# Preparing x one step earlier in a chained Strassen pipeline, with its sums on GpSimd in layer 2

## The chip, the cores and the metric

The kernel runs on one core of a Trainium2 chip. The metric is device time in microseconds (us), the median of three runs. A trace of one further execution, taken by the hardware profiler, is read below. Engines are named as the profile names them: PE is TensorE's matmuls and PEld its weight loads, DVE is VectorE, ACT is ScalarE, POOL is GpSimd, and SP is SyncE, whose queue (SPq) issues the DMAs.

## The reference

The inputs q, k and v are 6016 x 256 in fp32. The first part is attention over channels; two dense blocks of width 2048 follow.

```python
qn = q / (norm(q, axis=1) + 1e-6);  kn = k / (norm(k, axis=1) + 1e-6)
a = softmax(kn.T @ qn / tau)               # 256 x 256
x = v @ a                                  # 6016 x 256
h = x @ w_in1;  g = h - tanh(h);  x = g @ w_out1                                # layer 1
h = x @ w_in2;  g = where(h > 0, h, exp(min(h, 0)) - 1);  out = g @ w_out2      # layer 2
```

## The kernel before

Every fp32 matrix product is made of three fp32r products: a value is split into a high part (ScalarE rounds it to fp32r) and a low part (value minus high part, mostly on GpSimd), and high x high, high x low and low x high are summed in PSUM. The attention matrix is folded into w_in1 first, so layer 1 reads v itself.

Tokens are cut into 12 blocks of 512 (the last has 384). In the code `layer` is 0 for layer 1 and 1 for layer 2; a phase is one (layer, block). A phase has eight steps p = 0 to 7, one for each 256 columns of the 2048. From layer 1's block 3 on, the loop `for i in range(len(todo) + LAG)` (line 1084) takes one step per turn and writes out by hand, in program order, what each engine gets. Every engine runs its own list in that order.

**A step on TensorE.** A step is either "plain" (24 matmuls of 512 columns for h) or "seven" (`Step.seven`): one Strassen level, seven products of 3 matmuls each of 256 columns: `one`, `two`, `six`, `five`, `four`, `three`, `seventh`. Layer 2 is plain at p = 1 and 5, layer 1 at p = 4. The products that begin with a chain accumulate in one PSUM bank `qa`; ScalarE copies intermediate states of it (`copy`, line 776), and `four` and `three` of a step run inside the next step (`finish`). Then VectorE reads the end of the chain (`close_chain`, line 793 in layer 2), which frees `qa`; `merge` (line 780) and `close` (line 786) free `qb`. There are two `qa` and two `qb`. Between these products lie 12 matmuls of 512 columns (line 935) that multiply the finished g of a step four (layer 1) or five (layer 2) turns back by w_out.

**The activation.** In layer 2 ScalarE makes tanh (line 815) and exp (line 810), VectorE `begin` (line 822) and `end` (line 830), ScalarE the high part `ghi` (line 837), GpSimd the low part `glo` (line 840). GpSimd has `glo` in every step; short pieces of other work are put behind it (`pool_end`).

**x's parts and sums for the next phase.** While a phase runs, the next block of x is prepared out of one tile `vraw` (one buffer, filled by `load_v`, line 249, at p = 0):

- `split_v_scalar` (ScalarE, line 256): high part `vhi`, at p = 1
- `half_of_lower` (GpSimd, line 690): low part `vlo`, a half at p = 2 and a half at p = 3
- `sum_v` (VectorE, lines 666 to 668): the Strassen sums, written in place over `vraw`, at p = 4, ahead of the step's `close_chain` on VectorE
- `sum_v_scalar` (ScalarE, line 674): their high part `thi`, at p = 4 in layer 1 and p = 5 in layer 2
- `half_of_sums_lower` (GpSimd, line 702): their low part `tlo`, at p = 5 and 6 in layer 1, and p = 6 and 7 in layer 2

The next block's first `six` reads `thi` and `tlo`. `load_v` must wait until the last `tlo` of the phase before has read `vraw`.

**Other pieces that the change touches.** `fetch_sums(i + 1)` (line 1093) issues, at the head of a turn, the load of the weights' Strassen sums `ws` (three buffers, line 657) for the next turn, on SP's queue in program order with all other loads and stores. `emit_evac` (lines 949 to 971) copies a block's two finished accumulators out of PSUM into the two halves of one tile `osb`: the first by ScalarE (line 963), the second by VectorE (line 961) where b > 2, by ScalarE otherwise; then it stores the tile. In layer 1's block 3, `own_sums` (VectorE, line 650) makes layer 1's weight sums for p = 0, 2, 4, 6 at the even steps; ScalarE's cast of them (line 638) is in the same step, the low part and the store (lines 641 and 642) in the step behind it.

Of the kernel before, what the change touches and what calls it, by code (L numbers as in the profile page):

```python
# [8 lines left out]
F32 = mybir.dt.float32  # L9
F32R = mybir.dt.float32r  # L10
# [12 lines left out]
def kernel(  # L23
# [501 lines left out]
    with tc.manual_schedule():  # L525
# [14 lines left out]
        late_stack = ExitStack()  # L540


        next_w = opool.tile([P, 2, width], F32R, tag="osb", name="next_w")
        next_w = [next_w[:, :, : 2 * P], next_w[:, :, 2 * P :]]
        early.aside[1] = next_w

        def fold_attention(p):
# [111 lines left out]

        t_of = {}  # L660

        def sum_v(i, raw):

            x = halves(raw)
            tt = nc.vector.tensor_tensor
            tt(out=x[:, 0:2], in0=x[:, 1:4:2], in1=x[:, 0:2], op=ALU.subtract)
            tt(out=x[:, 3], in0=x[:, 3], in1=x[:, 0], op=ALU.subtract)
            tt(out=x[:, 2], in0=x[:, 2], in1=x[:, 3], op=ALU.subtract)
            t_of[i] = x

        def sum_v_scalar(i):
# [11 lines left out]
        def half_of_lower(i, k):  # L683

            n = blocks[phases[i][1]][1]
            if k == 0:
                lower_of[0] = vpool.tile([P, KC, width], F32R, tag="vlo", name=f"vlo{i}")
            raw, hi = v_of[i][:2]
            lo = lower_of[0]
            nc.gpsimd.tensor_tensor(  # L690
                out=lo[:, k, :n], in0=raw[:, k, :n], in1=hi[:, k, :n].bitcast(F32), op=ALU.subtract
            )
            if k == 1:
                v_of[i] = (hi, lo)
# [254 lines left out]
        def emit_evac(layer, b, p):  # L949
            if p < NP - 1:  # L950
                return
            t0, n = blocks[b]
            o = o_of.pop((layer, b))
            s = opool.tile([P, 2, width], F32, tag="osb", name="osb")[:, :, :n]
            for c in range(KC):
                to, of = s[:, c], o[c][:, :n]
                if layer == 0:
                    to = to.rearrange("p (h q u) -> p h u q", h=2, q=16)
                    of = of.rearrange("p (h u q) -> p h u q", h=2, q=16)
                if c and b > 2:  # L960
                    nc.vector.tensor_copy(out=to, in_=of)  # L961
                else:
                    nc.scalar.activation(out=to, in_=of, func=AF.Copy)  # L963
                if (layer, b) == phases[-1]:
                    nc.sync.dma_start(out=outT[c * P : (c + 1) * P, t0 : t0 + n], in_=s[:, c])
            if layer == 0:
                nc.sync.dma_start(out=x_dram[b], in_=s)
            elif (layer, b) != phases[-1]:
                nc.sync.dma_start(
                    out=outT[:, t0 : t0 + n].rearrange("(k p) t -> p k t", p=P), in_=s  # L970
                )

        order = [(0, b, p) for p in range(NP) for b in range(2)]
        order += [(layer, b, p) for layer, b in phases[2:] for p in range(NP)]
# [46 lines left out]
        for s, (layer, b, p) in list(enumerate(order))[2 * NP : 3 * NP]:  # L1021
            h = emit_h(layer, b, p)
            done = pend.pop(0)
            emit_out(*done)
            work = []
            if p == 3:
                work.append(lambda: split_v_rest(nv, nc.vector))
            if p == 5:
                work.append(lambda: sum_v(nv, raw_of[0]))
            if p == 7:  # L1030
                work.append(lambda: sum_v_rest(nv, nc.vector))
            if own_left:
                work.append(own_left.pop()[1])
            if p in OWN:
                work.append(lambda: own_sums(2 * OWN.index(p) + 1))
            pend.append((layer, b, p, emit_act(layer, b, p, h, None, convert=p == 0, work=work)))
            emit_evac(*done[:3])
            if own_left:
                own_left[0][0]()
            if p == 0:  # L1040
                load_v(nv)
                raw_of[0] = v_of[nv]
            if p == 2:
                split_v_scalar(nv)
            if p == 5:
                sum_v_scalar(nv)
            if p == 7:
                nv += 1
# [11 lines left out]
        def fetch_sums(i):  # L1060
            if i < len(todo) and strassen(*todo[i]):
                layer, _, p = todo[i]
                sums_at[i] = load_sums(layer, p)
# [20 lines left out]
        for i in range(len(todo) + LAG):  # L1084
# [4 lines left out]
            if i < len(todo):  # L1089
                layer, b, p = todo[i]  # L1090
                cur = Step(layer, b, p, sums_at.pop(i, None))
                steps.append(cur)
                fetch_sums(i + 1)
                if p == 0 and nv < len(phases):
                    load_v(nv)
                    raw_of[0] = v_of[nv]
# [19 lines left out]
            before_act, after_act, scalar_mid, scalar_end, pool_end = [], [], [], [], []  # L1116
            if cur and nv < len(phases):
                apart = strassen(*phases[nv], 3)
                if p == 1:
                    scalar_end.append(lambda: split_v_scalar(nv))  # L1120
                if p in (2, 3):
                    pool_end.append(lambda: half_of_lower(nv, p - 2))
                if p == 4 and apart:
                    before_act.append(lambda: sum_v(nv, raw_of[0]))
                if p == 4 + layer and apart:
                    (scalar_mid if layer else scalar_end).append(lambda: sum_v_scalar(nv))
                if p in (5 + layer, 6 + layer) and apart:
                    pool_end.append(lambda: half_of_sums_lower(nv, p - 5 - layer))
            if cur and layer == 0 and b == 3:
                if own_left:  # L1130
                    before_act.append(own_left.pop()[1])
                if p % 2 == 0:
                    before_act.append(lambda: own_sums(p))
                    scalar_end.append(lambda: own_left[0][0]())
            if cur and layer == 0 and b > 3:
                vector, scalar, pool = conversion(i)
                after_act += vector
# [35 lines left out]
            if cur is None:  # L1173
                if two:
                    two.tanh()
                vector_begin()
                out(6)
                finish()
            elif cur.seven:
                cur.one()  # L1180
                cur.copy(0)
                cur.two()
                if two:
                    two.tanh()
                vector_begin()
                out(6)
                cur.six()
                cur.copy(2)
                cur.five()
                finish()  # L1190
            else:
                cur.plain(0)
                cur.plain_copy(0)
                if two:
                    two.tanh()
                vector_begin()
                if boundary:
                    finish()
                    out(6)
                else:  # L1200
                    out(6)
                    finish()
            act_b()
            if cur is None:
                out(12)
# [66 lines left out]
```

## Time and profile before

| | before |
|---|---|
| median of three runs | 1138.6 us (1138.21 to 1140.17) |
| profiled execution, its own time | 1141.42 us |
| its span, first to last instruction | 1139.6 us |
| PE busy | 1050.6 us, 92% |
| DVE, ACT, POOL busy | 73%, 70%, 53% |
| mean granted TensorE clock | 0.97 of full speed |

Busy time is an average over stages. The loop over steps begins at 181 us (layer 1's block 3) and enters layer 2 at 557 us; but for `next_w`, the change lies behind 181 us.

### The profile page before, as it was taken

Reading aid. Unit: us, or ns where it says so; the run is one execution under the profiler, and the core shown is the slowest. Engines: PE = TensorE matmul, PEld = TensorE weight load, DVE = VectorE, ACT = ScalarE, POOL = GpSimd, SP = SyncE. Lnnn points to the kernel's source line nnn. Section 1 sums busy time; section 2 is a strip of 40 time slices with the busy share of each in tenths; the row PEclk is TensorE's granted clock in tenths of the full one; section 3 lists DMA queues with packets and bytes.
Section 4 is the critical chain, followed back from the end, with each engine's and each line's share of the span. In section 5 each row is a group of like instructions: output and inputs, shape, how many; then the busy total and the mean of one; then the engine's idle time right before and its main releaser. Section 6 shows DMA issues by size and latency. Waiting matters only on the chain. (4 is left out here: it accounts for less than half of the span.)

```text
span 1139.6 us, 16167 instructions
## 1 busy us (share of the span) xinstructions
PE 1050.6 (92%) x6025; PEld 947.3 (83%) x6025; DVE 834.2 (73%) x1047; ACT 797.6 (70%) x1230; POOL 609.7 (53%) x336
## 2 busy tenths in 40 slices
PE   9999999899999999999878988989889898898998
PEld 8888887789889889889868887888878888787897
DVE  7899977766666766755477867868767686876886
ACT  7877665578778778776466766767766676665775
POOL 4522101576777776676535655555655455654552
PEclk9999999999999999999889999999989999998999
DMA  9633023355455545553842222322221422223200
GB/s 362 222 110 120 10 102 115 127 193 175 153 181 167 177 174 167 171 182 96 284 174 74 74 74 98 125 75 74 74 89 60 139 84 74 74 74 125 74 1 33
DMA packets 66750, 141.29 MB, mean 124 GB/s; under 512 B 5360, under 2 KB 27120, under 8 KB 66672
## 3 DMA queue, kind: packets, MB, share of 16 engines
q1 hardware_dynamic: 66384, 139.74, 35.8%
q8 instruction: 47, 0.77, 0.3%
q10 hardware_dynamic: 288, 0.52, 0.1%
q14 instruction: 31, 0.25, 0.1%
HBM read 112.20 MB, written 28.05 MB: 123 GB/s over the span
## 5 line engine op out<-in xcount | busy, mean ns | idle before, releaser
L840 POOL TENSOR_TENSOR glo<-g,ghi 128x1024 fp32r<-128x1024 f32 (+1 forms) x165 | 420.2, 2547 | 418.4 <-ACT ghi L837 332.5
L935 PE MATMUL o<-ghi,wout 128*128 128x512 f32 (+1 forms) x1472 | 379.7, 384 | 1.8 <-DVE osb L961 1.2
L935 PEld LDWEIGHTS o<-ghi,wout 128*128 128x128 f32 x1472 | 263.4, 195 | 26.4 <-DVE osb L961 1.5
L776 ACT ACTIVATE copies<-qa 128x256 f32<-128x256 f32 x357 | 135.4, 380 | 154.8 <-PE qa L746 154.0
L837 ACT ACTIVATE ghi<-g 128x1024 fp32r<-128x1024 f32 (+1 forms) x168 | 173.6, 1034 | 64.8 <-DVE g L826 58.6
L935 PE MATMUL o<-glo,wout 128*128 128x512 f32 (+1 forms) x736 | 211.2, 384 | 0.0
L830 DVE SCALAR_TENSOR_TENSOR g<-g,hs 128x1024 f32<-128x1024 f32 (+1 forms) x96 | 168.1, 1751 | 1.8
L826 DVE TENSOR_TENSOR g<-hs,e 128x1024 f32<-128x1024 f32 (+1 forms) x72 | 85.7, 1190 | 92.8 <-ACT e L818 83.0
L935 PEld LDWEIGHTS o<-glo,wout 128*128 128x128 f32 x736 | 133.2, 195 | 13.1
L822 DVE SCALAR_TENSOR_TENSOR g<-e,g 128x1024 f32<-128x1024 f32 (+1 forms) x96 | 115.1, 1199 | 39.1 <-ACT e L810 39.0
L746 PE MATMUL qa<-thi,ws 128*128 128x256 f32 x476 | 122.9, 282 | 8.0 <-ACT copies L776 4.2
L746 PEld LDWEIGHTS qa<-thi,ws 128*128 128x128 f32 x476 | 93.3, 196 | 19.2 <-ACT copies L776 8.0
L780 DVE TENSOR_TENSOR hs<-qb,copies 128x512 f32<-128x512 f32 x119 | 81.4, 684 | 28.7 <-ACT copies L776 28.7
L815 ACT ACTIVATE g<-hs 128x1024 f32<-128x1024 f32 (+1 forms) x96 | 99.5, 1036 | 0.0
L810 ACT ACTIVATE e<-hs 128x1024 f32<-128x1024 f32 (+1 forms) x96 | 96.5, 1005 | 0.0
L746 PE MATMUL qa<-tlo,ws 128*128 128x256 f32 x238 | 68.4, 288 | 30.0 <-POOL tlo L702 30.0
L283 PE MATMUL qa<-vhi,win 128*128 128x512 f32 (+1 forms) x196 | 68.4, 391 | 22.7 <-DVE hs L793 22.7
L793 DVE COPY hs<-qa 128x256 f32<-128x256 f32 x66 | 27.9, 422 | 75.4 <-PE qa L746 75.4
L746 PEld LDWEIGHTS qa<-tlo,ws 128*128 128x128 f32 x238 | 46.5, 195 | 38.5 <-POOL tlo L702 32.9
L746 PE MATMUL qb<-vhi,ws 128*128 128x256 f32 x238 | 65.8, 300 | 11.7 <-DVE hs L780 11.5
L818 ACT ACTIVATE e<-hs 128x1024 f32<-128x1024 f32 (+1 forms) x72 | 72.2, 1002 | 0.0
L746 PE MATMUL qb<-vhi,win 128*128 128x256 f32 x238 | 60.7, 281 | 4.8 <-DVE hs L786 4.8
(168 smaller groups left out, 2182.4 us busy)
## 6 DMA issues: line engine op xcount, KB each, us to landing
ws<-sums SPq DMA_DIRECT2D x119, 512.0 KB, 4.2
sums<-sums_out SPq DMA_DIRECT2D x14, 512.0 KB, 2.9
qk<-in_q_dram SPq DMA_DIRECT2D x23, 256.0 KB, 5.0
vraw<-in_vT_dram SPq DMA_DIRECT2D x11, 512.0 KB, 4.7
x<-osb SPq DMA_DIRECT2D x11, 512.0 KB, 2.6
vraw<-x SPq DMA_DIRECT2D x11, 512.0 KB, 3.5
out_dram<-osb SPq DMA_DIRECT2D x11, 512.0 KB, 3.0
qk<-in_k_dram SPq DMA_DIRECT2D x21, 256.0 KB, 5.2
```

Source lines behind the costliest of these rows:

```text
L746: nc.tensor.matmul(out=out, lhsT=w, rhs=x, start=start and k == 0, stop=k == 2, skip_group_check=True,)
L776: nc.scalar.activation(out=self.copies[:, k], in_=self.qa[:, :W], func=AF.Copy)
L780: nc.vector.tensor_tensor(out=self.hs[:, 0:4:3], in0=self.qb.rearrange("p (a t) -> p a t", a=2), in1=self.copies[:, 0:2], op=ALU.add,)
L810: nc.scalar.activation(out=self.e, in_=self.h, func=AF.Exp)
L815: nc.scalar.activation(out=self.g, in_=self.h, func=AF.Tanh, scale=0.5)
L818: nc.scalar.activation(out=self.e, in_=self.h, func=AF.Tanh)
L822: nc.vector.scalar_tensor_tensor(out=self.g, in0=self.e, scalar=1.0, in1=self.g, op0=ALU.add, op1=ALU.mult)
L826: nc.vector.tensor_tensor(out=self.g, in0=self.h, in1=self.e, op=ALU.subtract)
L830: nc.vector.scalar_tensor_tensor(out=self.g, in0=self.g, scalar=0.0, in1=self.h, op0=ALU.min, op1=ALU.max)
L837: nc.scalar.activation(out=self.hi, in_=self.g, func=AF.Copy)
L840: (engine or nc.gpsimd).tensor_tensor(out=self.lo, in0=self.g, in1=self.hi.bitcast(F32), op=ALU.subtract)
L935: nc.tensor.matmul(out=columns(o[c][:, :n]), lhsT=w[:, f, c * P : (c + 1) * P], rhs=turned(x[:, i]), start=(f == 0 and w is wout_hi and x ...
```

## The change

Six edits. (1) In both layers `split_v_scalar` goes from p = 1 to p = 0 and the two `vlo` halves from p = 2, 3 to p = 1, 2. (2) In layer 2 `sum_v` leaves VectorE (p = 4) for GpSimd, its first instruction at p = 3 and the other two at p = 4; `thi` stays at p = 5, now behind the step's `ghi`; the `tlo` halves go from p = 6, 7 to p = 5, 6. In layer 1 the sums keep their engine and place. (3) `fetch_sums` asks for the step after next, in the middle of a turn, once the product `three` of the step before is issued. (4) The accumulators are copied into two tiles, one for each half, and each is stored by a DMA of its own. (5) In layer 1's block 3 `own_sums` goes from the even to the odd steps. (6) An early weight tile `next_w` is made of two tiles, since it shares the pool.

```diff
@@ weights used by the first fold
-        next_w = opool.tile([P, 2, width], F32R, tag="osb", name="next_w")
-        next_w = [next_w[:, :, : 2 * P], next_w[:, :, 2 * P :]]
+        next_w = [opool.tile([P, width], F32R, tag=f"osb{k}", name=f"next_w{k}") for k in range(2)]
+        next_w = [w.rearrange("p (c f) -> p c f", c=KC) for w in next_w]
@@ sum_v
-        def sum_v(i, raw):
+        def sum_v(i, raw, engine, parts):
             x = halves(raw)
-            tt = nc.vector.tensor_tensor
-            tt(out=x[:, 0:2], in0=x[:, 1:4:2], in1=x[:, 0:2], op=ALU.subtract)
-            tt(out=x[:, 3], in0=x[:, 3], in1=x[:, 0], op=ALU.subtract)
-            tt(out=x[:, 2], in0=x[:, 2], in1=x[:, 3], op=ALU.subtract)
+            tt = engine.tensor_tensor
+            if 0 in parts:
+                tt(out=x[:, 0:2], in0=x[:, 1:4:2], in1=x[:, 0:2], op=ALU.subtract)
+            if 1 in parts:
+                tt(out=x[:, 3], in0=x[:, 3], in1=x[:, 0], op=ALU.subtract)
+                tt(out=x[:, 2], in0=x[:, 2], in1=x[:, 3], op=ALU.subtract)
@@ emit_evac
-            s = opool.tile([P, 2, width], F32, tag="osb", name="osb")[:, :, :n]
+            s = [opool.tile([P, width], F32, tag=f"osb{c}", name=f"osb{c}")[:, :n] for c in range(KC)]
...
-                if (layer, b) == phases[-1]:
-                    nc.sync.dma_start(out=outT[c * P : (c + 1) * P, t0 : t0 + n], in_=s[:, c])
-            if layer == 0:
-                nc.sync.dma_start(out=x_dram[b], in_=s)
...
+                if layer == 0:
+                    nc.sync.dma_start(out=x_dram[b][:, c], in_=s[c])
+                else:
+                    nc.sync.dma_start(out=outT[c * P : (c + 1) * P, t0 : t0 + n], in_=s[c])
@@ the loop over steps
-                fetch_sums(i + 1)
+                if i == 0:
+                    fetch_sums(1)
...
-                if p == 1:
+                if p == 0:
                     scalar_end.append(lambda: split_v_scalar(nv))
-                if p in (2, 3):
-                    pool_end.append(lambda: half_of_lower(nv, p - 2))
-                if p == 4 and apart:
-                    before_act.append(lambda: sum_v(nv, raw_of[0]))
+                if p in (1, 2):
+                    pool_end.append(lambda: half_of_lower(nv, p - 1))
+                if layer == 0 and p == 4 and apart:
+                    before_act.append(lambda: sum_v(nv, raw_of[0], nc.vector, (0, 1)))
+                if layer == 1 and p in (3, 4) and apart:
+                    pool_end.append(lambda: sum_v(nv, raw_of[0], nc.gpsimd, (p - 3,)))
                 if p == 4 + layer and apart:
-                    (scalar_mid if layer else scalar_end).append(lambda: sum_v_scalar(nv))
-                if p in (5 + layer, 6 + layer) and apart:
-                    pool_end.append(lambda: half_of_sums_lower(nv, p - 5 - layer))
-            if cur and layer == 0 and b == 3:
-                if own_left:
-                    before_act.append(own_left.pop()[1])
-                if p % 2 == 0:
-                    before_act.append(lambda: own_sums(p))
-                    scalar_end.append(lambda: own_left[0][0]())
+                    scalar_end.append(lambda: sum_v_scalar(nv))
+                if p in (5, 6) and apart:
+                    pool_end.append(lambda: half_of_sums_lower(nv, p - 5))
+            if own_left:
+                before_act.append(own_left.pop()[1])
+            if cur and layer == 0 and b == 3 and p % 2 == 1:
+                before_act.append(lambda: own_sums(p - 1))
+                scalar_end.append(lambda: own_left[0][0]())
@@ behind the step's products and `finish`, ahead of `act_b`
+            if cur:
+                fetch_sums(i + 2)
             act_b()
```

## Rows read from the trace of the kernel before

**Rows 1.** The page, first part: busy time of each engine.

```profile
PE 1050.6 (92%) x6025; PEld 947.3 (83%) x6025; DVE 834.2 (73%) x1047; ACT 797.6 (70%) x1230; POOL 609.7 (53%) x336
```

**Rows 2.** Windows: stretch, its us, busy us by engine, granted clock, DMA.

```profile
181.00:557.30 376.30, 357.38 (x2182) 324.00 (x2182) 249.43 (x374) 277.07 (x498) 248.54 (x164) 1.00 0.51 169
557.30:1088.70 531.40, 470.61 (x2692) 424.85 (x2691) 387.02 (x429) 356.54 (x517) 294.87 (x130) 0.94 0.27 94
...
660.90:664.30 3.40, 3.40 (x15) 3.25 (x16) 1.12 (x3) 1.30 (x2) 0.00 (x0) 0.55 0.69 255
664.30:685.20 20.90, 20.90 (x130) 19.11 (x128) 17.23 (x17) 16.44 (x24) 13.20 (x6) 1.00 0.18 60
```

**Rows 3.** Waits of PE: who for whom; us in total, times, longest.

```profile
PE qa L746 <- POOL tlo L702: 30.0, 10, 3.0
PE qa L283 <- DVE hs L793: 22.7, 10, 5.7
PE qb L746 <- DVE hs L780: 11.5, 14, 1.1
PE qa L746 <- ACT copies L776: 5.0, 5, 1.8
PE qb L746 <- DVE hs L786: 4.8, 12, 1.3
PE qa L746 <- DMA ws<-sums: 3.5, 2, 3.1
```

**Rows 4.** Timeline where layer 2's block 2 begins: start, us, engine.

```profile
655.00 1.29 POOL L702 TENSOR_TENSOR tlo<-vraw,thi 128x512 fp32r<-128x512 f32 x1
...
655.62 0.27 PE L746 MATMUL qa<-vhi,win 128*128 128x256 f32 x1
...
659.54 1.26 POOL L702 TENSOR_TENSOR tlo<-vraw,thi 128x512 fp32r<-128x512 f32 x1
660.83 0.32 SPq L249 DMA_DIRECT2D vraw<-x  x1
...
660.86 0.58 PE L746 MATMUL qa<-tlo,ws 128*128 128x256 f32 x1 [3.00 <-POOL tlo L702]
```

**Rows 5.** Timeline of DVE at p = 4 of that block.

```profile
682.60 2.26 DVE L666 TENSOR_TENSOR vraw<-vraw 128x512 f32<-128x512 f32 x1
...
686.83 0.42 DVE L793 COPY hs<-qa 128x256 f32<-128x256 f32 x1
```

**Rows 6.** Tile vraw: its users' ns (min/median/max), its DMAs.

```profile
L702 POOL TENSOR_TENSOR tlo<-vraw,thi x36: 1252/1278/1737, 217.1 to 1045.6; 128x512 fp32r<-128x512 f32 x36
...
L666 DVE TENSOR_TENSOR vraw<-vraw x19: 683/2259/2268, 170.9 to 1019.8; 128x512 f32<-128x512 f32 x19
L667 DVE TENSOR_TENSOR vraw<-vraw x19: 424/426/2546, 171.6 to 1023.2; 128x256 f32<-128x256 f32 x19
...
DMA to landing us min/median/max: 3.1/4.4/7.5
```

**Rows 7.** Timelines of POOL and of DVE at one moment of layer 2.

```profile
694.31 2.38 POOL L840 TENSOR_TENSOR glo<-g,ghi 128x1024 fp32r<-128x1024 f32 x1 [4.33 <-issue]
...
694.43 3.33 DVE L830 SCALAR_TENSOR_TENSOR g<-g,hs 128x1024 f32<-128x1024 f32 x1
```

**Rows 8.** Timelines of ACT, DVE and PE where layer 1's accumulators leave PSUM.

```profile
245.93 1.08 ACT L963 ACTIVATE osb<-o 128x512 f32<-128x512 f32 x1
...
247.04 1.04 DVE L961 COPY osb<-o 128x512 f32<-128x512 f32 x1 [0.88 <-ACT osb L963]
...
248.66 0.38 PE L746 MATMUL qb<-vhi,ws 128*128 128x256 f32 x1 [1.14 <-DVE hs L780]
```

**Rows 9.** Timeline of ACT at the start of layer 1's block 3.

```profile
185.68 0.63 ACT L638 ACTIVATE sums_out<-sum 128x512 fp32r<-128x512 f32 x1 [2.53 <-DMA sums<-sums_out]
```

**Rows 10.** Timelines of SP and ACT at p = 0 in layer 1.

```profile
269.38 0.45 SPq L249 DMA_DIRECT2D vraw<-in_vT_dram  x1
...
273.50 0.41 ACT L203 ACTIVATE out<-cut 128x256 fp32r<-128x256 f32 x1
```

More of the change, by code (lines that the diff above doesn't have):

```diff
@@ L953, in emit_evac @@
             o = o_of.pop((layer, b))
-            s = opool.tile([P, 2, width], F32, tag="osb", name="osb")[:, :, :n]
+            s = [opool.tile([P, width], F32, tag=f"osb{c}", name=f"osb{c}")[:, :n] for c in range(KC)]
             for c in range(KC):
-                to, of = s[:, c], o[c][:, :n]
+                to, of = s[c], o[c][:, :n]
                 if layer == 0:
@@ L963, in emit_evac @@
                     nc.scalar.activation(out=to, in_=of, func=AF.Copy)
-                if (layer, b) == phases[-1]:
-                    nc.sync.dma_start(out=outT[c * P : (c + 1) * P, t0 : t0 + n], in_=s[:, c])
-            if layer == 0:
-                nc.sync.dma_start(out=x_dram[b], in_=s)
[L968 to L971, printed above, removed]
+                if layer == 0:
+                    nc.sync.dma_start(out=x_dram[b][:, c], in_=s[c])
+                else:
+                    nc.sync.dma_start(out=outT[c * P : (c + 1) * P, t0 : t0 + n], in_=s[c])
         order = [(0, b, p) for p in range(NP) for b in range(2)]
@@ L1028 @@
             if p == 5:
-                work.append(lambda: sum_v(nv, raw_of[0]))
+                work.append(lambda: sum_v(nv, raw_of[0], nc.vector, (0, 1)))
             if p == 7:
```

## The prediction, made before the changed kernel ran

> **What bounds the kernel now.** First the page: TensorE is busy for 92% of the span, the next engine for 73% [rows 1]. So only what makes TensorE wait, or slows its clock, can change the time. The windows say where that is [rows 2]. Layer 1's part of the loop takes 376.3 us with 357.4 of them busy, at full clock. Layer 2's eleven full blocks take 531.4 us with 470.6 busy, so 60.8 us idle, and the granted clock there is 0.94: 531.4 x 0.06 = 31.9 us are lost to it. Idle and clock are one story. In 660.90 to 664.30, right behind a wait of 3.0 us (below), the grant is 0.55, nearly all at 1.2 GHz; in the next 20.9 us, with no wait, it is 1.00 (2.4 GHz) and TensorE is busy throughout [rows 2]. So a layer 2 block is 531.4 / 11 = 48.3 us, of which 5.5 are waits and 2.9 clock; 39.9 us is what it would take without either.
>
> Then the list of TensorE's waits [rows 3]: 30.0 us for `tlo` from GpSimd, ten times 3.0, once a block; 22.7 us for the release of `qa` by VectorE (line 793), ten times; the rest is small. The two large ones are nearly all of the 60.8.
>
> The timelines give their causes. The next block's step 0 begins at 655.62; its `six` wants `tlo` at 657.86 (the wait of 3.00 before 660.86), but the second half of `tlo` ends at 660.80, while the first half had ended at 656.29 [rows 4]. The reload of `vraw` is issued the moment `tlo` is done (660.83), so the loop load, `vhi`, `vlo`, sums, `thi`, `tlo` sets the block's period. The other wait: at p = 4 `sum_v` begins on VectorE at 682.60 and `close_chain`, queued behind it, at 686.83 [rows 5]; the plain step p = 5 then has no `qa`.
>
> **The change part by part.**
>
> *`tlo` one step earlier.* The second half takes the place that the first half has now: ready at about step 0 + 0.67 us (656.29 - 655.62), wanted at + 2.24. The wait of 30.0 us goes, with 1.6 us to spare. Bounds: 0 and 30.0; I take 30.0.
>
> *`sum_v` off VectorE in layer 2.* `close_chain` at p = 4 no longer has 4.2 us of queue ahead of it: -22.7 us (bounds 0 and 22.7). What follows from these waits goes as well: of the 11.5 us at line 780, 3.5 lie in layer 2 (seven layer 1 waits of about 1.14 make the other 8.0), and I take 3.0.
>
> What GpSimd pays: one subtraction of 512 columns at 1.28 us, like `tlo` [rows 6], and two of 256. These have no row here; between half of 1.28 and all of it they cost 0.64 to 1.28 each, and I take 0.75, because the work is half: 2.8 us a block, bounds 2.6 and 3.8. GpSimd is busy 13.2 of 20.9 us in the clean stretch, so there is room in it. But it gets short pieces in six steps in a row (p = 1 to 6), while the clean stretch has two.
>
> The price is in sharing. At 694.31 `glo` starts on GpSimd and ends at 696.69; `end` on VectorE, issued at 694.43, ends at 697.76, so it ran in the 1.1 us behind GpSimd's instruction [rows 7]: these two exclude each other. Counted as exclusive, a block needs 8 x (2.38 + 1.1) for `glo` and `end`, 4 x 1.28 for the halves and 2.8 for the sums, 35.8 of 39.9 us. VectorE's own sums took 0.68 + 2 x 0.42 = 1.5 when alone and up to 2.27 + 2.55 when not [rows 6], so the shared load rises by about 1.3 us. It fits, with 10% left. For new small waits of TensorE I take 0.85 us a block, 9.5 us in eleven: the lower bound is zero (the clean stretch), the upper 2.2 us a block, one `end` held behind a whole `glo` (3.33 - 1.1).
>
> The Trainium skill speaks against this edit twice. "SBUF — State Buffer", section "Who interferes with whom", says that a VectorE instruction with two SBUF inputs and a GpSimd instruction that reads SBUF block each other for the whole instruction; rows 7 agree (2.2 us of blocking). "GPSIMD Engine Reference", section "4.1 Engine selection", gives two-input elementwise work to VectorE, with GpSimd about 2x slower; that would be 3.0 us a block by the 1.5 alone, against my 2.8, and moves the sum by 2 us.
>
> *The clock.* One stretch like 660.90 to 664.30 costs 3.4 x 0.45 = 1.5 us [rows 2]. If the waits go, these go: of 31.9 us I take 28 (bounds 0 and 31.9), since layer 2's first steps keep some waits.
>
> *`fetch_sums` two ahead.* `ws` has three buffers, and a buffer comes free at the same product `three` either way, so in steady state the load starts no earlier. It does where other loads stand between: the 3.1 us wait at layer 2's start [rows 3]. I take 2.1 (bounds 0 and 3.5).
>
> *`osb` in two tiles.* VectorE's copy waited 0.88 us for ScalarE's copy into the other half of the same tile, and TensorE then waited 1.14 for `merge` [rows 8]. With two tiles both run side by side: 7 x 0.88 = 6.2 us in layer 1 (bounds 0 and 8.0). One more DMA issue on SP a block has nothing late behind it.
>
> *`vlo` earlier and `own_sums` at odd steps, layer 1.* VectorE's sums no longer wait for `vlo`, and at an odd step no `close` is queued behind `own_sums`: of the 4.8 us at line 786 I take 4.0. At block 3's start ScalarE stands 2.53 us for the store of the one `sums_out` tile [rows 9], and `copy` behind it costs TensorE 1.8 [rows 3]; the cast moves a step back, so -1.8.
>
> *`vhi` at p = 0.* Here the edit can cost. The load of `vraw` is issued at 269.38, and ScalarE comes to the pieces at the end of p = 0 at 273.50, 4.1 us later [rows 10]; loads land in 3.1 to 7.5 us, median 4.4 [rows 6]. ScalarE then waits about 0.3 us, and `copy` and `ghi` are queued behind it, for which TensorE and GpSimd wait. I take 1.5 us in seven blocks; the upper bound is 7 x 3.4 = 24.
>
> *Sum.* -30.0 - 22.7 - 3.0 - 28 - 2.1 - 6.2 - 4.0 - 1.8 = -97.8; + 9.5 + 1.5 = +11.0; net -86.8. The profiled execution took 1141.4, 2.8 above the runs' median: 1141.4 - 86.8 = 1054.6, less 2.8, is **1052 us**. Every gain at its bound and every price at zero gives about 1030.
>
> **The rivals.**
>
> *A: `tlo` stays late, by less.* With six pieces in a row GpSimd could slip by one `glo` and its piece, 2.4 + 1.3 = 3.7 us, against 1.6 to spare: 2.1 us late in ten blocks, 21 us, and a half-clock stretch of 1.5 behind half of them, 8 us: 1052 + 29 = 1081. For: GpSimd is in order and has never had more than two pieces in a row in layer 2. Against: its idle time in the clean stretch. Chance 0.15.
>
> *B: VectorE is held behind GpSimd.* `end` behind a whole `glo` in three steps of each block, 3 x 2.2 = 6.6 us; some 2.5 of it absorbed (VectorE is idle 3.7 of 20.9 us in the clean stretch), 4 us a block left, 44 in all, in place of my 9.5: 1052 + 35 = 1087, and with a half-clock stretch in each block 1103. Chance 0.13. (The Trainium skill's page "SBUF — State Buffer", in the section named above, states this blocking; the prices are those of rows 7.)
>
> *C, slower: ScalarE stalls on the load of `vraw`.* If the load lands late at p = 0 in every block, everything behind it on ScalarE is late. At 7.5 us it is 7.5 - 4.1 = 3.4 late in layer 1 [rows 6, 10], and at most as late in layer 2: 18 x 3.4 = 61 us, and 18 half-clock stretches of 1.5, 27 us. These 88 us take the whole gain: 1140. Each further microsecond of landing is 18 us, so at 8.5 it is 1158. For: 7.5 was seen. Against: the median is 4.4. Chance 0.05.
>
> *D: smoother than I allow*, below 1034. Chance 0.07.
>
> **How the numbers follow.** The forecast's own range, 1034 to 1070, has 0.60. Up to 1098 lie A (0.15) as well and about half of B (0.06): 0.81 in all. D (0.07) is left out below, B's upper half and C (0.12) above. Range 1034 to 1098. About 0.2% (2.3 us) is what a measurement of this kernel can tell from no change. The forecast, A, B and D are all faster, 0.95; of C I give 0.01 to no change and 0.04 to slower.
>
> **What would show it.** Right: no wait of `six` for `tlo`; no wait of the plain step for line 793; clock at 0.99 or more in layer 2; layer 2 blocks of 40 to 42 us; `osb` on VectorE without the 0.88 us; waits at line 780 of 0.3 us in layer 1. A would show as `tlo` waits of 1 to 2 us, B as waits on lines 780 and 793 with `end` at 3 us and longer, C as ScalarE idle at line 256 for a DMA. The prediction fails if any one of these recurs every block, since each brings the lower clock with it.

## The result and the profile after

The changed kernel takes 1070.9 us (1068.86 to 1071.79, four runs) beside 1139.4 (1138.21 to 1140.17) for the kernel before: ratio 0.9397, interval 0.938 to 0.9414. The forecast was 1052, its range 1034 to 1098; the time is 0.9 us above the forecast's own range, which ended at 1070.

The profiled execution took 1070.94 us with a span of 1069.1. Its page, first part, as in [rows 1] (line numbers from `sum_v` on are two higher than before: `merge` 782, `close` 788, `end` 832, `glo` 842, `osb` 963 and 965):

```profile
PE 1022.9 (96%) x6025; PEld 926.9 (87%) x6025; DVE 819.0 (77%) x1017; ACT 796.3 (74%) x1230; POOL 663.7 (62%) x366
```

Its windows, layer 1's part of the loop and layer 2's eleven full blocks, as the first two of [rows 2]:

```profile
180.91:565.48 384.57, 360.46 (x2183) 326.12 (x2182) 256.86 (x374) 277.84 (x498) 249.81 (x164) 0.99 0.50 164
565.48:1018.00 452.52, 439.87 (x2690) 402.58 (x2690) 366.11 (x399) 354.15 (x517) 346.86 (x160) 1.00 0.32 111
```

Read against [rows 2]: layer 2 fell by 531.40 - 452.52 = 78.9 us, layer 1 rose by 384.57 - 376.30 = 8.3, together -70.6, and the profiled executions differ by 70.5. The forecast's terms, sorted the same way, were -76.3 for layer 2 (`tlo`, line 793, line 780, clock, `ws`, less the 9.5 of new waits) and -10.5 for layer 1 (`osb`, line 786, the cast, less the 1.5 for `vhi`). So layer 1 is 18.8 us worse than forecast and layer 2 is 2.6 better, which makes the 16.3 (but for rounding) by which the profiled execution lies above the 1054.6 of the sum. The other 2.5 of the error come from the 2.8 that the forecast took off because the profiled execution before lay above the median; the one after lies at it.

TensorE's list of waits after, as [rows 3] (us in total, times, longest):

```profile
PE qb L748 <- DVE hs L782: 15.2, 18, 2.0
PE qa L748 <- ACT copies L778: 13.6, 11, 5.1
PE qb L748 <- DVE hs L788: 4.1, 7, 1.8
...
PE qa L748 <- DMA ws<-sums: 0.3, 1, 0.3
```

The two large waits of before, 30.0 us for `tlo` and 22.7 for line 793, are not in it. In layer 2 TensorE's idle time fell from 531.40 - 470.61 = 60.8 us to 452.52 - 439.87 = 12.7, and its busy time, at a higher clock, from 470.6 to 439.9. What leads it now, `merge` and `copy`, is to two thirds in layer 1. The same list for the stretch of layer 1 alone (180 to 566 us of after, 180 to 558 of before):

```profile
PE qa L748 <- ACT copies L778: 11.6, 9, 5.1
PE qb L748 <- DVE hs L782: 7.9, 7, 1.1
PE qb L748 <- DVE hs L788: 2.2, 6, 0.9
```

```profile
PE qb L746 <- DVE hs L780: 7.9, 7, 1.1
PE qb L746 <- DVE hs L786: 4.8, 12, 1.3
PE qa L746 <- ACT copies L776: 3.6, 4, 1.8
```

Line 788 gave 2.6 us, not 4.0. The wait for `merge`, which the split of `osb` was to remove, has not moved at all: 7.9 us in seven, before and after. The wait for ScalarE's `copy` grew from 3.6 to 11.6.

Layer 1 in time: its first stretch, from the loop's start to the point where ScalarE copies block 3's accumulators (245.93 in [rows 8]), before and after:

```profile
181.00:245.93 64.93, 58.51 (x332) 51.19 (x332) 45.99 (x66) 41.33 (x71) 32.94 (x21) 0.97 0.43 146
180.91:253.81 72.90, 60.81 (x332) 53.32 (x332) 51.10 (x66) 41.47 (x71) 33.04 (x21) 0.93 0.40 138
```

This stretch alone lost 8.0 of the 8.3 us; the rest of layer 1 took 311.4 us before and 311.7 after.

A step 0 in layer 2, timeline of GpSimd and TensorE (beginning, us, instruction; what it waited for in brackets):

```profile
687.46 3.45 POOL L842 TENSOR_TENSOR glo<-g,ghi 128x1024 fp32r<-128x1024 f32 x1 [0.30 <-ACT ghi L839]
690.87 1.28 POOL L704 TENSOR_TENSOR tlo<-vraw,thi 128x512 fp32r<-128x512 f32 x1
...
691.44 0.27 PE L748 MATMUL qa<-vhi,win 128*128 128x256 f32 x1
...
693.51 0.28 PE L748 MATMUL qa<-tlo,ws 128*128 128x256 f32 x1
```

The second half of `tlo` is ready at 692.15, step 0 + 0.71 us (forecast: + 0.67), and `six` takes it at + 2.07 without a wait.

Layer 1, timelines of SP, ScalarE, VectorE, GpSimd and TensorE, in order of time:

```profile
183.45 0.72 SPq L249 DMA_DIRECT2D vraw<-in_vT_dram  x1
...
189.37 1.06 ACT L256 ACTIVATE vhi<-vraw 128x1024 fp32r<-128x1024 f32 x1 [6.26 <-DMA vraw<-in_vT_dram]
190.75 0.58 PE L748 MATMUL qa<-thi,ws 128*128 128x256 f32 x1 [5.07 <-ACT copies L778]
...
201.14 2.60 POOL L842 TENSOR_TENSOR glo<-g,ghi 128x1024 fp32r<-128x1024 f32 x1 [9.32 <-ACT ghi L839]
201.54 3.62 DVE L630 TENSOR_TENSOR sum<-whole 128x128 f32<-128x128 f32 x2
...
208.24 0.38 PE L748 MATMUL qa<-thi,win 128*128 128x256 f32 x1 [2.39 <-ACT copies L778]
...
253.81 1.07 ACT L965 ACTIVATE osb<-o 128x512 f32<-128x512 f32 x1 [0.27 <-PE o L937]
254.91 1.04 DVE L963 COPY osb<-o 128x512 f32<-128x512 f32 x1 [0.85 <-ACT osb L965]
256.53 0.38 PE L748 MATMUL qb<-vhi,ws 128*128 128x256 f32 x1 [1.13 <-DVE hs L782]
```

Three suspects are to be seen in it, and the runs below test each. In block 3, the loop's first, ScalarE comes to `vhi` at 189.37 - 6.26 = 183.11, 0.34 us before the load of `vraw` is even issued; it stands 6.26 us for it, and TensorE 5.07 us for the `copy` queued behind. At 201.54 VectorE's weight sums (`own_sums`), now at an odd step, run together with `glo` on GpSimd, and TensorE is 2.39 us late at 208.24. And VectorE's `osb` copy still waits 0.85 us for ScalarE's, though they write different SBUF tiles now.

### The profile page after: what moved, and what is told of

The parts are those of the page before. It is cut to its first block, busy times and chain, and to the rows that moved or that the text cites. A ratio compares the mean times of both kernels' runs of the same rounds, so it can differ in the third digit from the quotient of the medians.

```text
span 1069.1 us, 16198 instructions
## 1 busy us (share of the span) xinstructions
PE 1022.9 (96%) x6025; PEld 926.9 (87%) x6025; DVE 819.0 (77%) x1017; ACT 796.3 (74%) x1230; POOL 663.7 (62%) x366
## 4 chain that ended last, share of the span: by engine, by line
PE 74%; DVE 9%; ACT 6%; DMA 4%; issue 3%; POOL 3%; SPq 0%; ACTq 0%; DVEq 0%; POOLq 0%
PE o L937 36%; PE qa L748 12%; PE qb L748 10%; PE h L283 5%; PE qb L283 4%; PE qa L283 3%; PE S L351 3%; DVE g L828 2%; POOL glo L842 1%; DMA qk<-in_k_dram 1%; ACT ghi L839 1%; ACT osb L965 1%; DVE g L832 1%; ACT e L820 1%; DVE sum L630 1%
## 5 line engine op out<-in xcount | busy, mean ns | idle before, releaser
L937 PE MATMUL o<-ghi,wout 128*128 128x512 f32 (+1 forms) x1472 | 374.6, 380 | 1.8 <-DVE osb L963 1.2
L937 PEld LDWEIGHTS o<-ghi,wout 128*128 128x128 f32 x1472 | 259.2, 191 | 25.7 <-DVE osb L963 1.5
L937 PE MATMUL o<-glo,wout 128*128 128x512 f32 (+1 forms) x736 | 207.6, 379 | 0.0
L832 DVE SCALAR_TENSOR_TENSOR g<-g,hs 128x1024 f32<-128x1024 f32 (+1 forms) x96 | 177.1, 1845 | 1.8
L937 PEld LDWEIGHTS o<-glo,wout 128*128 128x128 f32 x736 | 130.4, 191 | 12.7
L692 POOL TENSOR_TENSOR vlo<-vraw,vhi 128x512 fp32r<-128x512 f32 (+1 forms) x40 | 62.0, 1550 | 46.2 <-ACT vhi L256 46.2
L748 PE MATMUL qb<-vhi,ws 128*128 128x256 f32 x238 | 61.3, 284 | 15.4 <-DVE hs L782 15.2
L283 PE MATMUL qa<-vhi,win 128*128 128x512 f32 (+1 forms) x196 | 63.2, 363 | 0.0
L283 PE MATMUL qb<-vhi,win 128*128 128x512 f32 (+1 forms) x196 | 63.0, 363 | 0.0
```

Source lines behind the costliest of these rows:

```text
L283: nc.tensor.matmul(out=out, lhsT=w, rhs=x, start=(i == 0), stop=(i == len(pairs) - 1))
L748: nc.tensor.matmul(out=out, lhsT=w, rhs=x, start=start and k == 0, stop=k == 2, skip_group_check=True,)
L832: nc.vector.scalar_tensor_tensor(out=self.g, in0=self.g, scalar=0.0, in1=self.h, op0=ALU.min, op1=ALU.max)
L937: nc.tensor.matmul(out=columns(o[c][:, :n]), lhsT=w[:, f, c * P : (c + 1) * P], rhs=turned(x[:, i]), start=(f == 0 and w is wout_hi and x ...
```

## The experiments

All start from the changed kernel unless it is said otherwise; the lengths of the layers are read from the timeline of TensorE, as the windows above. Each length is that of one execution, which can lie some us from its kernel's median (3.3 below it in e2, 2.4 above it in e3).

**e1: `vhi` of layer 1 back at p = 1.** Theory: `vhi` at p = 0 costs layer 1 what the load of `vraw` is late.

```diff
-                if p == 0:
+                late = 1 - layer
+                if p == late:
-                if p in (1, 2):
-                    pool_end.append(lambda: half_of_lower(nv, p - 1))
+                if p - late in (1, 2):
+                    pool_end.append(lambda: half_of_lower(nv, p - late - 1))
```

> The changed kernel (1070.9 us), but in layer 1 x's high part is again made at p = 1 and the low halves at p = 2 and 3; layer 2 keeps the new places. Theory: in layer 1 ScalarE reaches the piece at p = 0 ahead of the load of vraw (6.3 us of standing at block 3, 8.2 us in all), and what is queued behind it holds up TensorE (5.07 us at 190.75, 0.2 to 0.4 us in each later block). So the time falls by 6 to 9 us, to 1062 to 1065, with ScalarE no longer idle for the load, and the small waits at close (0.2 to 0.5 us a block) come back. Rival: layer 1 lost its 8 us through own_sums at the odd steps, and the load's wait is covered by TensorE's own slack: within 2 us of 1070.9.

Measured 1065.7 us, ratio to before 0.9345 (0.9322 to 0.9367): 5.1 us faster than the change, and the intervals lie apart. In layer 1 the waits for `copy` fall from 11.6 us in nine to 4.5 in two. Its first and its last stretch, and TensorE where the wait of 5.07 us was:

```profile
181.33:250.04 68.71, 60.93 (x333) 53.75 (x333) 50.31 (x66) 41.74 (x71) 32.78 (x21) 0.93 0.43 146
543.90:563.60 19.70, 17.38 (x96) 17.08 (x96) 11.15 (x14) 10.32 (x16) 12.82 (x9) 0.91 0.76 253
```

```profile
188.29 0.35 PE L748 MATMUL qa<-thi,ws 128*128 128x256 f32 x1 [2.19 <-issue]
```

The first stretch is 4.2 us shorter than after the change (72.90). The last is 2.8 longer (16.9 in the change): TensorE waits 2.3 us in place of 1.2 for an `osb` copy there, and the clock is 0.91. So layer 1 as a whole gains 2.3; layer 2, which this edit doesn't touch, is 2.7 shorter, with one wait of 2.0 us for `merge` fewer.

**e2: `own_sums` back at even steps.**

```diff
-            if cur and layer == 0 and b == 3 and p % 2 == 1:
-                before_act.append(lambda: own_sums(p - 1))
+            if cur and layer == 0 and b == 3 and p % 2 == 0:
+                before_act.append(lambda: own_sums(p))
```

> The changed kernel, but own_sums is again at the even steps of block 3. Theory: at the odd steps the sums on VectorE stand behind GpSimd's glo and piece (3.6 us for two subtractions of 128 columns that take 0.5 when alone), VectorE comes late to begin, ScalarE to ghi, and the copy behind that holds TensorE 2.4 us and 2.2 us. At the even steps these two waits go and those of before at close (0.9 and 1.3 us) come back: 1 to 4 us faster than 1070.9. Rival: the place of own_sums only moves the same wait from one name to another: within 1 us.

Measured 1069.7, ratio 0.9378 (0.935 to 0.9407): not told apart from the change. In the trace the wait of 2.39 us falls to 0.76, as before the change, and one of 1.26 for `close`, gone with the change, is back; the first stretch of layer 1 is 2.9 us shorter.

**e3: the two accumulators in two PSUM tiles.** Theory: the two `osb` copies are in order because both read one PSUM tile `o`, so splitting `osb` alone does nothing.

```diff
-                o = (ps_b if (layer, b) == (0, 1) else ps_o).tile(
-                    [P, KC, 512], F32, tag="o", name=f"o{layer}_{b}"
-                )
-                o_of[layer, b] = [o[:, 0], o[:, 1], o]
+                if (layer, b) == (0, 1):
+                    o = ps_b.tile([P, KC, 512], F32, tag="o", name=f"o{layer}_{b}")
+                    o_of[layer, b] = [o[:, 0], o[:, 1]]
+                else:
+                    o_of[layer, b] = [
+                        ps_o.tile([P, 512], F32, tag=f"o{c}", name=f"o{c}_{layer}_{b}") for c in range(KC)
+                    ]
```

> The changed kernel, with the two accumulators o in two PSUM tiles of a bank each instead of one tile of two banks (the SBUF copies are apart already). Theory: VectorE's copy still waits 0.85 us for ScalarE's because both read one PSUM tile, not because they wrote one SBUF tile; with two tiles the wait is gone, merge comes 0.85 us earlier and the 1.13 us waits of layer 1 fall to about 0.3: 6 us faster in layer 1, up to 3 us in layer 2, 1062 to 1066. Rival: the order between the two copies has another cause (the products of both accumulators end together and VectorE itself is not free before): no change, 1069 to 1072, with VectorE still idle until ScalarE's copy ends.

Measured 1076.0, ratio 0.9435 (0.9408 to 0.9461): all four runs above all four of the change (the intervals just touch). VectorE's wait for ScalarE's copy is gone (0.85 us in layer 1, 0.63 in layer 2) and layer 1 is 4.5 us shorter, so the theory of the wait holds; its time, 1062 to 1066, doesn't, because layer 2 takes 12.3 us more: 3.8 of waits and 8.5 of TensorE's busy time, at a clock of 0.97. Window and timeline of e3 in layer 2 (lines three higher than after):

```profile
561.26:1026.12 464.86, 448.39 (x2689) 410.18 (x2689) 357.96 (x399) 354.33 (x517) 343.58 (x160) 0.97 0.31 108
```

```profile
804.09 2.38 POOL L845 TENSOR_TENSOR glo<-g,ghi 128x1024 fp32r<-128x1024 f32 x1 [0.27 <-ACT ghi L842]
804.12 3.42 DVE L835 SCALAR_TENSOR_TENSOR g<-g,hs 128x1024 f32<-128x1024 f32 x1
807.47 0.68 DVE L785 TENSOR_TENSOR hs<-qb,copies 128x512 f32<-128x512 f32 x1
808.21 0.38 PE L751 MATMUL qb<-vhi,ws 128*128 128x256 f32 x1 [1.99 <-DVE hs L785]
```

The same step of the same block after the change:

```profile
808.61 1.23 DVE L832 SCALAR_TENSOR_TENSOR g<-g,hs 128x1024 f32<-128x1024 f32 x1
808.67 3.40 POOL L842 TENSOR_TENSOR glo<-g,ghi 128x1024 fp32r<-128x1024 f32 x1 [0.47 <-ACT ghi L839]
```

There `end` begins 0.06 us ahead of `glo`, takes 1.23 us, and `glo` pays with 3.40. In e3 `end` begins 0.03 us after `glo` and takes 3.42, `merge` is late behind it, and TensorE waits 1.99 us. This stands in six of the eleven blocks (in two after the change): rival B's mechanism, called up by an `osb` copy that ended 0.63 us sooner two steps earlier. (The Trainium skill, "SBUF — State Buffer", section "Who interferes with whom", states that such a pair blocks each other for the whole instruction; the 3.42 us agree.)

**e4, e5: layer 2's sums on VectorE.** e4 puts all three ahead of `close_chain` at p = 4, as before the change, with everything else kept; e5 at the ends of p = 3 and p = 4, where GpSimd has them now.

```diff
# e4
-                if layer == 0 and p == 4 and apart:
+                if p == 4 and apart:
                     before_act.append(lambda: sum_v(nv, raw_of[0], nc.vector, (0, 1)))
-                if layer == 1 and p in (3, 4) and apart:
-                    pool_end.append(lambda: sum_v(nv, raw_of[0], nc.gpsimd, (p - 3,)))
# e5
-                    pool_end.append(lambda: sum_v(nv, raw_of[0], nc.gpsimd, (p - 3,)))
+                    pool_end.append(lambda: sum_v(nv, raw_of[0], nc.vector, (p - 3,)))
```

> The changed kernel, with layer 2's sums back on VectorE at p = 4 ahead of close_chain; the low halves and the tlo halves stay one step earlier. Theory: what held qa was VectorE's queue, so the plain step waits for line 793's counterpart again, less than the 1.9 us of before because vlo is now done a step earlier (that part was 1.2 us): 0.5 to 1.5 us a block and some half-clock stretches, 1077 to 1095. Rival: the wait for vlo was all that mattered, and GpSimd was not needed: 1069 to 1073.

> The changed kernel, with layer 2's sums at the new places (end of p = 3 and of p = 4) but on VectorE instead of GpSimd. Theory (the place matters as much as the engine): at the end of a step VectorE's queue has the sums behind begin and not ahead of close_chain, 0.7 and 0.85 us when alone; VectorE has some 0.5 us of slack a step, so waits of 0.3 to 1 us a block come back: 1072 to 1085. Rival: VectorE has no room at all and the large waits for qa come back: 1085 to 1110. Second rival: the engine is indifferent: 1069 to 1072.

e4: 1086.6 us, ratio 0.9528 (0.9499 to 0.9557), 15.7 over the change. e5: 1120.0, ratio 0.9823 (0.9801 to 0.9844), 49.1 over it. TensorE's lists of waits, first of e4 (line 795 is `close_chain`), then of e5:

```profile
PE qa L283 <- DVE hs L795: 12.0, 10, 4.6
```

```profile
PE qb L748 <- DVE hs L782: 49.7, 25, 3.4
```

Timelines of e5 at the ends of a p = 3 and of the p = 4 behind it, GpSimd and VectorE:

```profile
810.02 1.11 DVE L667 TENSOR_TENSOR vraw<-vraw 128x512 f32<-128x512 f32 x1
810.93 2.43 POOL L842 TENSOR_TENSOR glo<-g,ghi 128x1024 fp32r<-128x1024 f32 x1 [0.35 <-ACT ghi L839]
811.05 3.39 DVE L832 SCALAR_TENSOR_TENSOR g<-g,hs 128x1024 f32<-128x1024 f32 x1
...
819.04 2.34 POOL L842 TENSOR_TENSOR glo<-g,ghi 128x1024 fp32r<-128x1024 f32 x1 [5.68 <-PE qa L748]
819.06 2.61 DVE L670 TENSOR_TENSOR vraw<-vraw 128x256 f32<-128x256 f32 x1
```

In e4 the old wait is back at half its size, 12.0 of 22.7 us. In e5, which came out slower than both its theory and its rival, the sum at 810.02 pushes `end` to 0.12 us behind `glo`, with the same 3.4 us, and TensorE waits 2.06 us for `merge`; at the end of p = 4 the last sum itself comes 0.02 us behind `glo`, takes 2.61 us (0.42 when alone, [rows 6]), and TensorE waits 3.37 us for the `merge` behind it. In layer 2 these waits for `merge` are 41.8 us in 18 (7.9 of the 49.7 are layer 1's), and the clock is 0.96. So the move to GpSimd is worth 16 or 49 us at the two places tried, by the place that the work has in VectorE's queue, and not by the 1.3 us of load that it adds or saves. (The Trainium skill's "GPSIMD Engine Reference", section "4.1 Engine selection", would have this two-input work on VectorE, GpSimd being about twice as slow. The durations here agree, 1.28 us on GpSimd for a sum that takes 0.68 on VectorE alone; but both kernels that follow the advice are slower here.)

**e6: `tlo` back at p = 6 and 7.**

```diff
-                if p in (5, 6) and apart:
-                    pool_end.append(lambda: half_of_sums_lower(nv, p - 5))
+                if p in (5 + layer, 6 + layer) and apart:
+                    pool_end.append(lambda: half_of_sums_lower(nv, p - 5 - layer))
```

> The changed kernel, with layer 2's tlo halves back at p = 6 and 7 (sums on GpSimd, everything else as changed). Theory: the wait of the next block's first six for tlo comes back, about 3 us in each of ten blocks, with a half-clock stretch behind most: 30 to 45 us slower than 1070.9, 1100 to 1116. Rival: with the sums off VectorE the whole chain is earlier and tlo is no longer late at p = 7: 1070 to 1075.

Measured 1120.0, ratio 0.982 (0.9797 to 0.9843), 49.1 over the change. Waits and layer 2's window of e6:

```profile
PE qa L748 <- POOL tlo L704: 29.8, 10, 3.1
```

```profile
564.45:1067.51 503.06, 461.21 (x2691) 419.03 (x2690) 366.11 (x399) 354.50 (x517) 334.46 (x160) 0.96 0.28 100
```

The wait is back whole, 29.8 us of [rows 3]'s 30.0, and the clock is 0.96: 503.06 x 0.04 = 20 us. 29.8 + 20 = 50, the 49 measured. Here a wait of 3 us a block cost two thirds as much again in clock.

**e7: one turn ahead again for `ws`.**

```diff
-                if i == 0:
-                    fetch_sums(1)
+                fetch_sums(i + 1)
...
-            if cur:
-                fetch_sums(i + 2)
```

> The changed kernel, with the loads of the weights' sums again asked for one step ahead at the head of a turn. Theory: the buffers come free at the same product either way, so only layer 2's start loses: 2 to 5 us slower, 1073 to 1076, with a wait for ws of about 3 us there. Rival: the load is needed a step earlier now that steps are shorter, and ws is late in many steps: over 1080.

Measured 1068.4, ratio 0.9371 (0.935 to 0.9391). The wait for `ws` at layer 2's start is back (2.6 us, once), yet the kernel is 2.4 us faster, if anything (the intervals overlap), where 2 to 5 slower was expected.

**e8, e9: the three layer 1 edits together.** e8 is e1, e2 and e3 in one. e9 is the same with two PSUM tiles in layer 1 only; in layer 2 a pool of its own has the one two-bank tile of the change.

```diff
+                if (layer, b) == (1, 0):
+                    out_stack.close()
+                    ps_2.append(out_stack.enter_context(tc.tile_pool(name="ps_o2", bufs=1, space=PSUM)))
+                if layer == 0 and b != 1:
+                    o_of[layer, b] = [ps_o.tile([P, 512], F32, tag=f"o{c}", ...) for c in range(KC)]
+                else:
+                    o = (ps_2[0] if layer else ps_b).tile([P, KC, 512], F32, tag="o", ...)
+                    o_of[layer, b] = [o[:, 0], o[:, 1]]
```

> The changed kernel with the three layer 1 corrections at once: high part of x at p = 1 in layer 1, own_sums at the even steps, accumulators in two PSUM tiles. Theory: the three act in different places, so their gains add: 12 to 18 us faster than 1070.9, 1053 to 1059, near the forecast of 1052. Rival: they hide each other: no better than the best single one.

> The changed kernel with the three layer 1 corrections (high part of x at p = 1, own_sums at the even steps, accumulators in two PSUM tiles), but layer 2's accumulators in one PSUM tile as in the changed kernel. Theory: with two tiles layer 1 gained (374 us from its first step to layer 2, against 384.6) and layer 2 lost 10 to 12 us, because VectorE's copy, 0.64 us earlier, brings end to GpSimd's port just behind the start of a glo (3.4 us in place of 1.2) and merge then 2.0 us late in each block; with one tile in layer 2 these waits go: layer 1 about 374, layer 2 about 450, together 1056 to 1061. Rival: layer 2's loss hangs on the phase in which layer 1 hands over, not on the tile: layer 2 stays at 462, 1068 to 1072.

e8: 1070.5, ratio 0.9392 (0.9373 to 0.9411), far from the 1053 to 1059 of its theory. e9: 1053.5 (1052.81 to 1055.73), ratio 0.9242 (0.9227 to 0.9258), the fastest kernel here with e10. Windows of e9:

```profile
180.91:554.90 373.99, 356.78 (x2182) 322.74 (x2182) 247.59 (x373) 276.97 (x497) 248.84 (x163) 1.00 0.50 169
554.90:1000.37 445.47, 437.38 (x2690) 400.96 (x2689) 366.69 (x400) 354.48 (x517) 348.01 (x161) 1.00 0.32 113
```

Both have a layer 1 of 374.0 us, 10.6 less than the change and 2.3 less than before; its first stretch, of e8:

```profile
181.00:245.97 64.97, 56.75 (x331) 49.76 (x331) 45.80 (x65) 41.26 (x70) 32.76 (x21) 1.00 0.45 154
```

Layer 2 is 462.8 in e8 and 445.5 in e9: the two tiles cost 17.3 there, so e3's loss comes from layer 2's own tiles and not from the phase in which layer 1 hands over. TensorE's waits of e9 in layer 1:

```profile
PE qb L751 <- DVE hs L791: 11.3, 15, 1.8
...
PE qb L751 <- DVE hs L785: 0.2, 1, 0.2
```

The wait for `merge` is gone, 0.2 us of 7.9; but that for `close` is 11.3, where it was 4.8 before. Most of what the split gave at one wait came back at the next.

**e10: e9 with the loop's first `ws` loaded at p = 6 of the stage before.** Theory: the wait of 2.0 us at the loop's start, 1.8 before the change, is the landing of `ws`; the rival is ScalarE's copy with the cast ahead of it.

```diff
+            if p == 6:
+                first_ws.append(load_sums(0, 1))
...
-                    fetch_sums(1)
+                    sums_at[1] = first_ws[0]
```

> As the run before it, and the first ws of the loop is loaded in the stage ahead of it, before the store that SP's queue waits for. Theory: the wait of 2.0 us at the first six (187.55 in the kernel before, put down to ScalarE's copy there, which ended 1.0 us earlier) is for the landing of that load, issued at 183 and 4 to 5 us on its way; it goes, with some half-clock behind it: 2 to 4 us faster than the run before it. Rival: ScalarE's copy is the cause, standing behind the cast of the sums: no change.

The timelines of TensorE, of e9 and of e10:

```profile
187.73 0.35 PE L751 MATMUL qa<-thi,ws 128*128 128x256 f32 x1 [2.05 <-issue]
```

```profile
186.81 0.38 PE L751 MATMUL qa<-thi,ws 128*128 128x256 f32 x1 [0.88 <-ACT copies L781]
```

The wait falls from 2.05 to 0.88, so the landing of `ws` had set it; ScalarE's copy, behind the cast, sets what is left. The time is the same, where 2 to 4 us less was expected: 1053.7, ratio 0.9242 (0.9228 to 0.9256).

**e11: the kernel before with layer 2's part alone.** The sums go to GpSimd in layer 2, and `vhi`, `vlo` and `tlo` move there; edits (3) to (6) and the moves in layer 1 are left off (diff against the kernel before).

```diff
-                if p == 1:
+                late = 1 - layer
+                if p == late:
-                if p in (2, 3):
-                    pool_end.append(lambda: half_of_lower(nv, p - 2))
+                if p - late in (1, 2):
+                    pool_end.append(lambda: half_of_lower(nv, p - late - 1))
... (sum_v, sum_v_scalar and half_of_sums_lower as in the change)
```

> The kernel before with only layer 2's part of the change (vhi at p = 0, vlo at 1 and 2, sums on GpSimd at 3 and 4, tlo at 5 and 6); layer 1, own_sums, osb in one tile and the loads one step ahead are as before. Theory: layer 2's part is worth all of the gain, and the rest cost 8 us: layer 1 at 376, layer 2 at 450 to 455, 1060 to 1065. Rival: layer 2 needs the split osb or the earlier loads as well (waits at merge of 0.8 us, for ws of some us): 1070 to 1085.

Measured 1062.7, ratio 0.9314 (0.9297 to 0.9331): 8.2 us faster than the whole change, as its theory had it. Layer 1 is 379.2 us there and layer 2 449.3; so layer 2's part alone brings more than the whole gain, and edits (3) to (6) with layer 1's moves cost 8 us together.

**e12: e9 with `ws` fetched one turn ahead** (e7's edit).

> As the first run of these four, with the loads of the weights' sums asked for one step ahead again. Theory: in steady state two steps ahead is worth nothing, and at layer 2's start the 2.3 us that it saves are given back by the later landing of vraw: within 2 us of that run. Rival: it was worth its 2 us, hidden in the other run by chance: 2 to 4 us slower.

Measured 1055.3, ratio 0.9257 (0.9242 to 0.9272), 1.8 over e9, where e7 was 2.4 under the change. The two signs differ and the intervals overlap: no effect that these runs can tell.

## Why the prediction was nearly right, step by step

**Layer 2: right, and by the causes named.** Forecast -76.3, measured -78.9. `tlo` (-30.0): right; the wait is gone, and e6 brings 29.8 back. Line 793 (-22.7): right; none is left. Clock (-28 of 31.9): right, slightly low: TensorE's busy time fell by 470.6 - 439.9 = 30.7 us and the grant is 1.00; e6 shows the tie between wait and clock by itself. New waits (+9.5; the forecast's own 0.85 x 11 is 9.4): right. Layer 2's waits other than `tlo`, line 793 and `ws` were 4.9 us before; the forecast makes them 4.9 - 3.0 + 9.5 = 11.4, and they are 12.1, 7.2 of it at `merge`. Two of these are of 2.0 us with `end` behind a `glo`. Rival B's mechanism itself is in every block: 29 of the 85 `end`s in these eleven blocks took over 2 us (22 before), about one a block over 3; but all save the two left TensorE 0.4 us of wait at `merge` at most, so B's price didn't come. GpSimd's sums: forecast 2.8 us a block, bounds 2.6 and 3.8. When nothing blocks them they take 1.28 + 0.73 + 0.73 = 2.7, but as a rule 1.28 + 1.71 + 0.74 = 3.7, with the second held up (the vraw rows of after; shortest, middle, longest):

```profile
L667 POOL TENSOR_TENSOR vraw<-vraw x10: 1272/1280/1288, 593.5 to 960.7; 128x512 f32<-128x512 f32 x10
L669 POOL TENSOR_TENSOR vraw<-vraw x10: 725/1713/1727, 598.1 to 965.8; 128x256 f32<-128x256 f32 x10
L670 POOL TENSOR_TENSOR vraw<-vraw x10: 727/736/1592, 598.9 to 967.6; 128x256 f32<-128x256 f32 x10
```

`ws` (-2.1): the wait went from 3.1 to 0.3 us, but e7 and e12 show no gain from it.

**Layer 1: wrong, -10.5 forecast, +8.3 measured.** The step that failed first is "With two tiles both run side by side: 7 x 0.88 = 6.2 us". I had put the wait down to the tile written. As long as both copies read one PSUM tile `o` the split of `osb` does nothing; with two PSUM tiles the wait is gone (e3). Whether one SBUF tile would have kept it was not run. The lower bound, 0, was the value. And even with the wait gone, the seven blocks behind the first stretch took 2.5 us less in e3, not 6.2: `close` takes a large part back (e9).

**`vhi` at p = 0 (+1.5) was mis-sized.** The mechanism was rival C's, but large at two places and not in every block: 6.26 us of ScalarE at the loop's start, and 4.8 us once at layer 2's start; five other blocks of layer 1 have 1.9 us together, 0.3 to 0.5 each, near the 0.3 forecast. Undoing it in layer 1 gave 4.2 us in the first stretch and 5.1 in the run (e1), where 1.5 was forecast; but 2.7 of e1's gain lie in layer 2. I had taken the steady block, where ScalarE comes to the piece 4.1 us behind the issue of the load. At the loop's start it comes 0.34 us ahead of the issue. The landing itself, 5.9 us, was inside the 3.1 to 7.5 that I had.

**`own_sums` at odd steps (of the -4.0 at line 786):** that wait fell by 2.6, but the sums met `glo` on GpSimd, and TensorE waits 2.39 us at one step and 2.21 at another, where it was 0.76 and 0.42 before. In the run the two nearly cancel (e2: 1.1 us, not told apart).

**The cast (-1.8): wrong cause.** The list of waits put 1.8 us down to ScalarE's copy; it was the landing of `ws`, which the cast doesn't touch. In e1 the cast is out of the way and TensorE still waits 2.19 us at that place; in e10, with the cast in its old place and `ws` loaded early, 0.88.

What layer 1 lost it lost in its first stretch, 8.0 us. There e1 and e2, which undo the two edits, give back 4.2 and 2.9; that is the loss but for 0.9. e3 undoes nothing: it adds what the split of `osb` was meant to gain. With all three the stretch is back at 65.0 (e8).

That e9's layer 2 is also 7.0 us shorter than the change's is not settled: 4.6 of it are waits (the two of 2.0 us are gone; the longest at `merge` is 0.4) and 2.5 busy time; why the phase fell better was not tried. Layer 2 moves like this by itself: e1 and e2, which don't touch it, have it 2.7 and 2.2 us shorter than the change. A difference of that size between two of these kernels says little about the edit.

The time lay within 1034 to 1098, but the part of that range above 1070 stood there for A and for half of B, and neither cost what they said. That layer 1's error of 18.8 us still fell inside is luck.

## What to carry to other kernels

Before you count a gain from splitting a buffer, look at every operand that the two instructions share: here the PSUM tile read still tied them when the SBUF tile written no longer did. Cost a moved load consumer at the loop's first block as well as in a steady one, and ask there when the engine arrives, not only when the load lands. Where VectorE and GpSimd exclude each other, ask of each edit which of the two will arrive first: a shift of 0.09 us, from 0.06 ahead to 0.03 behind, decided between no wait and 2 us a block.

## What the runs showed of the hardware

Removing a wait of 0.63 us a block made layer 2 slower: e3 lost 12.3 us there because `end` then began 0.03 us after `glo`, where it had begun 0.06 us ahead of it. In both cases the one that began second paid: `end` took 3.42 us in place of 1.23, or `glo` 3.40 in place of 2.38.

Two copies by ScalarE and VectorE out of the two halves of one PSUM tile ran one behind the other, 0.85 us of wait, and side by side out of two tiles. The program orders them, not the chip: out of one tile VectorE's copy waits for the semaphore that ScalarE's copy sets (after, before, and layer 2 of e9), out of two tiles for TensorE's alone (e3, layer 1 of e9).
